# The last layer's weight conversion begins at step 9 of the experts instead of step 0

## The chip, the cores and the metric

One core of a Trainium2 chip runs the whole program. The metric is device time in microseconds (us), as the median of the runs that a table below gives. One further execution was recorded by the hardware profiler; all rows below are from it.

## The reference

Three stages follow one another. Sparse attention (4 batches, 8 heads, 576 rows, 64 columns) gives 2304 tokens of 512 numbers. A mixture of 8 experts sends each token to one expert (argmax of a gate) and applies two layers with a relu between, 512 to 1024 to 512. A last layer of two matrices, 512 to 2048 to 512, is shared by all tokens:

```python
def _moe2_ref(x, w_in, w_out) -> np.ndarray:
    h = x @ w_in
    g = h - np.tanh(h)
    return (g @ w_out).astype(np.float32)
```

`w_in` and `w_out` are float64. The kernel gets them as pairs of 32-bit words and makes float32 numbers of them on the chip. That making is the conversion which the change moves.

## The kernel before

The change touches the stage of the experts. It runs in steps, g = 0 to 71: nine passes of eight steps, one pass per expert and two for the second largest group (steps 8 to 23). A pass handles N = 256, 256, 288, 416, 384, 336, 320, 288 and 272 tokens in turn, and a step one eighth of the hidden width. The last layer's 96 steps follow (`GE` is 72, so its numbers are counted from there).

In a step the loop of `run` issues, in this order: the first-layer product of step g on TensorE (`h_exp`, L982, twelve matmuls, since each factor is split in a high and a low part); the relu, on ScalarE (L1017) and VectorE (L1018, the low part); whatever the table of `plan` holds for this step; then the second-layer product of step g-2 (`y_exp`, L1037). Each engine works through what it was given in the order of issue. Nothing overtakes.

The table holds:

- `gather_exp` (L999): rows of tokens by an indirect transfer that GpSimd issues, ten steps ahead of a pass.
- `trans` and `evac` (L959, L969, L973): the gathered rows are transposed by TensorE into PSUM and taken out by ScalarE (L969) and VectorE (L973), seven steps ahead, so at steps 1, 2 and 3 of the pass before. There is one PSUM bank "t" for it: a second transpose waits until L973 has read the first.
- `wload` and `wsplit` (L944 or L933, L950, L952): 512 KB of weights are loaded by the SP queue, cast by ScalarE and split, first-layer weights by VectorE on even steps, second-layer weights by GpSimd on odd ones. "raw" has four buffers.
- the tables of positions and gates (`route_late`, L523 and others), every second step from 8 to 30.
- `conv`, 32 times: half a block of the float64 words. Four jobs at steps g, g+3, g+4, g+5: load (SP, L1078), `bits` (VectorE: L1088, L1090, L1092), `sign` (ScalarE L1096, VectorE L1097, GpSimd L1099), store to `wscr` (SP, L1102). "cv" has three buffers. `conv` comes last in the table of a step.
- `"last"`: when the converted blocks are read back and split.

At the end of a pass `y_exp` copies its four results out (L1040), two by ScalarE and two by VectorE ("yo"). These copies are issued in the second step of the next pass, behind all that the table held for that step, and the pass after needs the banks one step later. "h" has two banks in PSUM: the first-layer product of step g+2 waits for L1018 of step g.

Of the kernel before, what the change touches and what calls it, by code (L numbers as in the profile page):

```python
# [863 lines left out]
class Mlp(Moe):  # L864
# [315 lines left out]
    def early(self):  # L1180
# [3 lines left out]


    TB = {"wl": (4, 5), "ws": (2, 3), "ga": 10, "tr": 7, "ev": 7,
          "last": ((-3, -2), (-1, 1), (-2, 0), (0, 2), (-1, 2), (0, 3), (1, 2), (4, 6), (-60, -55), (-53, -50), (-7,
                  -1), (-6, -4), (5, 10), (9, 11), (11, 12), (12, 14)), "x0": (12, 9, 7), "x": (14, 13, 8),
          "conv": (0, 1, 3, 5, 7, 10, 11, 13, 15, 16, 18, 20, 21, 23, 25, 28, 29, 32, 33, 35, 37, 38, 40, 42, 44, 46,
                  47, 51, 52, 54, 57, 57), "cv": (0, 3, 4, 5), "eng": "DPDPDPDPDPPDDDPP"}  # L1190

    def plan(self, K):
        at = self.at
# [82 lines left out]
```

## Times and profile before

| what | value |
|---|---|
| median of 3 runs | 1124.69 us (1124.59 to 1127.33) |
| profiled execution: its own time | 1123.74 us |
| profiled execution: span | 1122.0 us |
| TensorE matmul busy | 989.8 us, 88% |
| TensorE weight load busy | 916.7 us, 82% |
| VectorE busy | 901.3 us, 80% |
| ScalarE busy | 643.5 us, 57% |
| GpSimd busy | 716.9 us, 64% |

The span runs from the first to the last instruction; the execution's own time is 1.74 us more. Shares are means over the attention (to about 380 us), the experts (about 402 to 695 us) and the last layer. Shares say which engine has room; which wait ends last in a stretch is read from the timeline.

### The profile page before, as it was taken

To read this page: it belongs to the slowest core of one execution; us is meant where nothing else is said; L and a number is where in the kernel's file an instruction comes from. 1 tells how busy PE (TensorE), PEld (TensorE's weight loads), DVE (VectorE), ACT (ScalarE), POOL (GpSimd) and SP (SyncE) were. 2 spreads that over 40 slices of the span, in tenths; PEclk is the share of its full clock that TensorE was granted. 3 is DMA by queue.
4 is the path that set the end of the run, shared out by engine and by line. 5 is a ranking of instruction groups with operands and counts; after the bars stand their busy time and mean duration, and the time that the engine had idled before them with its cause. 6 is when DMAs were issued, how large, how long until landed. Compare 5 with 4: busy or idle time off the path is not lost.

```text
span 1122.0 us, 23396 instructions
## 1 busy us (share of the span) xinstructions
PE 989.8 (88%) x8729; PEld 916.7 (82%) x8729; DVE 901.3 (80%) x1600; ACT 643.5 (57%) x1207; POOL 716.9 (64%) x538
## 2 busy tenths in 40 slices
PE   4769698788887677999999998989999999999997
PEld 3669688777787567989999998877999999999986
DVE  4969687877679359885979876988988989898894
ACT  5768677667676044433445546665566666566662
POOL 3958667757766046555555657776776767677673
PEclk9789889989899679999999999999999999999999
DMA  7999999999999576686778875320010101000000
GB/s 176 172 190 201 218 198 204 214 176 192 201 171 177 130 244 208 236 281 216 250 248 278 283 254 192 112 85 8 36 29 20 46 10 36 19 29 1 13 17 29
DMA packets 249778, 162.68 MB, mean 145 GB/s; under 512 B 180122, under 2 KB 222508, under 8 KB 249661
## 3 DMA queue, kind: packets, MB, share of 16 engines
q1 hardware_dynamic: 245901, 150.36, 56.4%
q0 software_dynamic: 3312, 10.49, 2.7%
q8 instruction: 70, 1.15, 0.4%
q14 instruction: 47, 0.39, 0.1%
q10 hardware_dynamic: 448, 0.30, 0.1%
HBM read 85.08 MB, written 23.60 MB: 97 GB/s over the span
## 4 chain that ended last, share of the span: by engine, by line
PE 45%; DVE 13%; issue 3%; ACT 2%; DMA 1%; POOL 0%; DVEq 0%; POOLq 0%; SPq 0%; ACTq 0%
PE h L982 22%; PE y L1056 14%; PE y L1037 8%; DVE w L1162 2%; DVE w L1163 2%; DVE cv L1090 2%; DVE cm L1088 1%; DVE w L1164 1%; DVE w L1160 1%; DMA xr<-rows,idx 1%; DVE w L952 1%; DVE cm L1092 1%; PE t L959 1%; ACT w L950 1%; DVE hbuf L1018 0%
## 5 line engine op out<-in xcount | busy, mean ns | idle before, releaser
L233 POOL TENSOR_TENSOR e<-em,e 128x1536 f16<-128x1536 f32 (+1 forms) x53 | 155.6, 2936 | 89.1 <-ACT e L229 61.6
L263 PE MATMUL ops<-vv,et 128*128 128x64 bf16 (+1 forms) x1440 | 143.6, 202 | 9.7 <-DVE x L269 5.4
L263 PEld LDWEIGHTS <-et 128*128 128x128 f16 (+1 forms) x3680 | 134.9, 107 | 19.7 <-issue 8.4
L221 DVE SCALAR_TENSOR_TENSOR em<-sps,n,e 128x576 f32<-128x576 f32 x144 | 116.6, 810 | 40.6 <-ACT e L208 39.5
L1159 POOL TENSOR_SCALAR tm<-u 128x384 uint8<-128x384 f32 x80 | 117.3, 1466 | 49.9 <-ACT u L1155 49.3
L982 PE MATMUL h<-xa,w 128*128 128x256 f32 (+6 forms) x864 | 142.2, 315 | 7.0 <-DVE hbuf L1018 5.0
L1037 PE MATMUL y<-hbuf,w 128*128 128x256 f32 (+6 forms) x864 | 141.0, 312 | 5.6 <-DVE yo L1040 5.6
L263 PE MATMUL ops<-vr,et 128*128 128x64 bf16 (+1 forms) x2240 | 142.0, 201 | 0.0
L982 PEld LDWEIGHTS h<-xa,w 128*128 128x128 f32 x864 | 132.5, 197 | 9.1 <-DVE hbuf L1018 5.9
L229 ACT CAST e<-em 128x576 f16<-128x576 f32 x144 | 97.1, 675 | 64.8 <-DMA et<-e 60.6
L1037 PEld LDWEIGHTS y<-hbuf,w 128*128 128x128 f32 x864 | 128.0, 191 | 7.0 <-DVE yo L1040 6.6
L202 DVE TENSOR_REDUCE n<-sps 128x1 f32<-128x576 f32 x144 | 107.5, 747 | 29.9 <-PE sps L194 28.7
L952 POOL TENSOR_TENSOR w<-raw,w 128x1024 fp32r<-128x1024 f32 x36 | 91.6, 2545 | 60.6 <-ACT w L950 32.2
L1162 DVE SCALAR_TENSOR_TENSOR w<-y,w 128x384 f32<-128x384 f32 x96 | 124.1, 1293 | 0.0
L1155 ACT ACTIVATE u<-h 128x384 f32<-128x384 f32 x96 | 47.1, 491 | 119.8 <-PE h L982 119.7
L208 ACT ACTIVATE e<-sps,n 128x576 f32<-128x576 f32 x144 | 107.9, 749 | 13.1 <-DVE n L202 11.9
L982 PE MATMUL h<-xk,w 128*128 128x384 f32 x576 | 109.8, 339 | 0.4 <-DVE tm L1161 0.2
L982 PEld LDWEIGHTS h<-xk,w 128*128 128x128 f32 x576 | 103.1, 189 | 5.0 <-DVE tm L1161 0.5
L1176 POOL TENSOR_TENSOR gl<-w,gh 128x384 fp32r<-128x384 f32 x83 | 85.5, 1031 | 30.4 <-ACT gh L1175 30.3
L1017 ACT ACTIVATE hbuf<-h 128x256 fp32r<-128x256 f32 (+6 forms) x72 | 31.1, 432 | 125.5 <-PE h L982 125.5
L194 PE MATMUL sps<-ka,qa 128*128 128x288 f32 x320 | 86.1, 362 | 8.6 <-DVE em L221 4.3
L1056 PE MATMUL y<-w,gh 128*128 128x512 f32 x258 | 82.3, 400 | 5.6 <-DVE yo L1040 4.1
(217 smaller groups left out, 2296.3 us busy)
## 6 DMA issues: line engine op xcount, KB each, us to landing
raw<-in_moe_w_dram SPq DMA_DIRECT2D x64, 512.0 KB, 5.1
qb<-qa SPq DMA_DIRECT2D x30, 304.0 KB, 4.3
cv<-in_moe_w_in_dram SPq DMA_DIRECT2D x16, 512.0 KB, 4.7
cv<-in_moe_w_out_dram SPq DMA_DIRECT2D x16, 512.0 KB, 4.5
wscr<-cm SPq DMA_DIRECT2D x32, 256.0 KB, 2.4
raw<-wscr SPq DMA_DIRECT2D x16, 512.0 KB, 4.1
xw<-yT SPq DMA_DIRECT2D x24, 192.0 KB, 2.3
vv<-in_v_dram SPq DMA_DIRECT2D x8, 512.0 KB, 5.2
```

What stands on the lines that cost most here:

```text
L202: nc.vector.tensor_reduce(out=n[:, 0:1], in_=ps[:, :, 0:288], axis=AX.XY, op=ALU.max, negate=True)
L208: nc.scalar.activation(out=e, in_=ps[:, :, 0:288], func=AF.Exp, bias=n[:, 0:1])
L221: nc.vector.scalar_tensor_tensor(out=self.em[u, g][:, i].rearrange("p (a b) -> p a b", a=2), in0=ps[:, :, 0:288], scalar=n[:, 1:2], in1=e, ...
L229: self.nc.scalar.copy(self.e16[u, g][:, i, 0:S], self.em[u, g][:, i])
L233: eng.tensor_tensor(out=e16[:, r, S + 64:], in0=em[:, r, 0:512], in1=e16[:, r, 0:512], op=ALU.subtract)
L263: nc.tensor.matmul(o[q], lhsT=et[:, base + c, q], rhs=vb[a][:, j, c if c < 5 else c - 5, :], start=(n == 0), stop=(n == len(terms) - 1))
L952: (self.nc.gpsimd if pool else self.nc.vector).tensor_tensor(out=l, in0=raw, in1=h.bitcast(F32), op=ALU.subtract)
L982: self.nc.tensor.matmul(out, lhsT=a, rhs=b, start=(i == 0), stop=(i == len(parts) - 1))
L1037: nc.tensor.matmul(self.ys[d], lhsT=a[:, f % 2, s], rhs=b, start=(f == 0 and i == 0), stop=(f == 7 and i == 2))
L1056: nc.tensor.matmul(self.ys[m], lhsT=a[:, s], rhs=b[:, f % 2], start=(f == 0 and i == 0), stop=(f == 15 and i == 2))
L1159: nc.gpsimd.tensor_scalar(out=mk, in0=u, scalar1=RCUT * RCUT, scalar2=None, op0=ALU.is_gt)
L1162: V.scalar_tensor_tensor(out=w, in0=y, scalar=b, in1=w, op0=ALU.add, op1=ALU.mult)
```

## The change

Only numbers in the table `TB` are changed: the steps of the 32 conversions, and the steps at which the first two converted blocks are read back and split.

```diff
-          "last": (..., (4, 6), (-60, -55), (-53, -50), (-7,
+          "last": (..., (4, 6), (-51, -47), (-46, -43), (-7,
...
-          "conv": (0, 1, 3, 5, 7, 10, 11, 13, 15, 16, 18, 20, 21, 23, 25, 28, 29, 32, 33, 35, 37, 38, 40, 42, 44, 46,
-                  47, 51, 52, 54, 57, 57), "cv": (0, 3, 4, 5), "eng": "DPDPDPDPDPPDDDPP"}
+          "conv": (9, 10, 12, 13, 15, 16, 18, 19, 21, 23, 24, 26, 27, 29, 30, 32, 33, 35, 37, 38, 40, 41, 43, 44,
+                   46, 48, 49, 51, 52, 54, 55, 57), "cv": (0, 3, 4, 5), "eng": "DPDPDPDPDPPDDDPP"}
```

The two pairs of "last" are the load and the split of block 4 of `w_in` (before: steps 12 and 17, after: 21 and 25) and of block 4 of `w_out` (before: 19 and 22, after: 26 and 29). The first is split by VectorE, the second by GpSimd.

## Rows read from the trace of the kernel before

**Rows 1.** The page: the chain that ended last, by engine.
```profile
PE 45%; DVE 13%; issue 3%; ACT 2%; DMA 1%; POOL 0%; DVEq 0%; POOLq 0%; SPq 0%; ACTq 0%
```
**Rows 2.** Busy us by stretch (instructions in brackets), then granted clock and DMA.
```profile
core 0: us, PE busy (x) PEld busy (x) DVE busy (x) ACT busy (x) POOL busy (x), PEclk, DMA share, GB/s
421.13:449.50 28.37, 21.01 (x159) 20.15 (x158) 27.70 (x39) 12.37 (x26) 17.23 (x11) 0.94 0.64 211
...
461.01:490.26 29.25, 27.75 (x211) 26.91 (x209) 26.23 (x45) 12.78 (x27) 13.72 (x10) 1.00 0.80 263
...
503.34:567.03 63.69, 63.69 (x378) 62.91 (x376) 47.96 (x72) 28.83 (x51) 34.17 (x20) 1.00 0.72 237
567.03:600.88 33.85, 31.84 (x206) 31.27 (x206) 26.42 (x38) 15.95 (x29) 18.73 (x12) 1.00 0.82 279
```
**Rows 3.** Timeline of PE, steps 6 to 13: start, duration, idle before in brackets.
```profile
421.13 1.60 PE L982 MATMUL h<-xa,w 128*128 128x256 f32 x12
...
425.63 1.70 PE L982 MATMUL h<-xa,w 128*128 128x256 f32 x12 [1.47 <-DVE hbuf L1018]
...
434.37 0.63 PE L959 MATMUL t<-ident,xr 128*128 128x128 f32 x4 [1.28 <-DMA xr<-rows,idx]
...
442.67 0.79 PE L959 MATMUL t<-ident,xr 128*128 128x128 f32 x4 [4.61 <-issue]
443.11 2.91 PE L1037 MATMUL y<-hbuf,w 128*128 128x256 f32 x12
...
449.50 1.60 PE L982 MATMUL h<-xa,w 128*128 128x256 f32 x12
...
452.38 1.60 PE L982 MATMUL h<-xa,w 128*128 128x256 f32 x12
```
**Rows 4.** Timeline of DVE and POOL in the same stretch.
```profile
422.12 2.83 POOL L952 TENSOR_TENSOR w<-raw,w 128x1024 fp32r<-128x1024 f32 x1
...
422.75 2.50 DVE L1092 TENSOR_SCALAR cm<-cv 128x512 f32<-128x512 f32 x1
...
441.82 0.74 DVE L973 TENSOR_TENSOR xa<-t,xa 128x384 fp32r<-128x384 f32 x2
```
**Rows 5.** Tile cm: VectorE's four operations (min/median/max ns); last, its busy us, 408.87 to 663.45.
```profile
L1088 DVE TENSOR_SCALAR cm<-cv x32: 409/420/2648, 414.9 to 656.0; 128x512 uint32<-128x512 uint32 x32
L1090 DVE SCALAR_TENSOR_TENSOR cv<-cv,cm x32: 692/694/2879, 415.3 to 656.5; 128x512 uint32<-128x512 uint32 x32
L1092 DVE TENSOR_SCALAR cm<-cv x32: 426/428/2812, 416.1 to 657.2; 128x512 f32<-128x512 f32 x32
...
L1097 DVE SCALAR_TENSOR_TENSOR cm<-cv,cm x32: 673/682/3553, 420.0 to 660.6; 128x512 f32<-128x512 f32 x32
...
sum 254.58, PE 0.00 PEld 0.00 DVE 118.46 POOL 42.84; mean PE 0.00 PEld 0.00 DVE 14.81 POOL 5.36
```
**Rows 6.** Timeline of steps 22 to 26.
```profile
488.10 2.49 POOL L952 TENSOR_TENSOR we<-raw,we 128x1024 fp32r<-128x1024 f32 x1 [3.62 <-ACT we L950]
488.25 2.70 DVE L523 TENSOR_TENSOR keep<-keep,tok 128x324 f16<-128x324 f32 x1
...
494.04 2.76 DVE L1092 TENSOR_SCALAR cm<-cv 128x512 f32<-128x512 f32 x1
...
497.36 4.09 PE L982 MATMUL h<-xa,w 128*128 128x416 f32 x12 [2.49 <-DVE hbuf L1018]
...
503.34 2.44 PE L982 MATMUL h<-xa,w 128*128 128x416 f32 x12
```
**Rows 7.** Waits of PE from 403 to 690 us: total, times, longest.
```profile
PE y L1037 <- DVE yo L1040: 5.6, 4, 2.2
PE h L982 <- DVE hbuf L1018: 5.0, 4, 2.5
```
**Rows 8.** Timeline of PE and DVE at step 34.
```profile
543.71 2.35 PE L1037 MATMUL y<-hbuf,w 128*128 128x384 f32 x12
...
543.80 1.07 DVE L1040 COPY yo<-y 128x416 f32<-128x416 f32 x2
```

More of the change, by code (lines that the diff above doesn't have):

```diff
@@ L1186 @@
     TB = {"wl": (4, 5), "ws": (2, 3), "ga": 10, "tr": 7, "ev": 7,
-          "last": ((-3, -2), (-1, 1), (-2, 0), (0, 2), (-1, 2), (0, 3), (1, 2), (4, 6), (-60, -55), (-53, -50), (-7,
+          "last": ((-3, -2), (-1, 1), (-2, 0), (0, 2), (-1, 2), (0, 3), (1, 2), (4, 6), (-51, -47), (-46, -43), (-7,
                   -1), (-6, -4), (5, 10), (9, 11), (11, 12), (12, 14)), "x0": (12, 9, 7), "x": (14, 13, 8),
-          "conv": (0, 1, 3, 5, 7, 10, 11, 13, 15, 16, 18, 20, 21, 23, 25, 28, 29, 32, 33, 35, 37, 38, 40, 42, 44, 46,
-                  47, 51, 52, 54, 57, 57), "cv": (0, 3, 4, 5), "eng": "DPDPDPDPDPPDDDPP"}
+          "conv": (9, 10, 12, 13, 15, 16, 18, 19, 21, 23, 24, 26, 27, 29, 30, 32, 33, 35, 37, 38, 40, 41, 43, 44,
+                   46, 48, 49, 51, 52, 54, 55, 57), "cv": (0, 3, 4, 5), "eng": "DPDPDPDPDPPDDDPP"}
     def plan(self, K):
```

## The prediction

> **What bounds the kernel now.** I read the chain of waits first. TensorE has 45% of the chain and VectorE 13%, far ahead of ScalarE and DMA [rows 1]: the kernel goes at TensorE's pace, broken by places where TensorE waits for VectorE. Then the stretches of the expert stage, the only stage in which conversions run [rows 2]. From 503.34 to 567.03 us TensorE is busy for all of the 63.69 us, and VectorE's 47.96 us of work cost nothing. From 421.13 to 449.50 us, steps 6 to 11, it is the other way round: VectorE is busy for 27.70 of 28.37 us and TensorE for 21.01. So the question is which waits fall in such stretches, and whether the conversion is in front of them.
>
> The timeline of TensorE in that stretch shows three waits [rows 3]: 1.47 us before step 7 (for L1018), 1.28 us before the first transposes (for gathered rows), 4.61 us before the second ones. After the last, y of step 8 takes 2.91 us, where a product of this width takes 1.60: the granted clock of the stretch is 0.94 [rows 2]. VectorE's and GpSimd's rows name the cause [rows 4]. The wait of 1.47 ends after L1092, a conversion's operation, which took 2.50 us beside GpSimd's split of 2.83 us. The wait of 4.61 us is put down to "issue", but it ends at 442.67 us, just as L973 ends (441.82 + 0.74 = 442.56): the single bank "t" was not read yet, since L973 stood in VectorE's queue behind conversions and the table of positions. The gather that TensorE waited 1.28 us for is issued by GpSimd, whose queue had conversion multiplies in front of it.
>
> **The change part by part.** Price of a conversion first. Its four VectorE operations have medians of 0.420, 0.694, 0.428 and 0.682 us, 2.22 together; their real total is 118.46 us for 32 conversions, 3.70 each [rows 5]. The 1.48 us between is time in which they stood blocked beside GpSimd.
>
> Counting `bits` per pass, before: 3, 4, 5, 4, 4, 5, 4, 3, 0; after: 0, 3, 5, 5, 5, 6, 5, 3, 0. Most of the conversions stay within a step or two of their place. In effect five leave steps 3 to 10 and come in at steps 12 to 15, 29, 33, 44 to 46 and 52.
>
> *Steps 6 to 11, removed.* The five that leave take 5 x 3.70 = 18.5 us of VectorE out of steps 3 to 11. What TensorE needs for steps 6 to 11: a step takes 452.38 - 449.50 = 2.88 us [rows 3], six make 17.28; three groups of transposes at 443.11 - 442.67 = 0.44 make 1.32; together 18.6. They took 28.37. So up to 9.8 us go. What is late next: the table of positions still stands at step 8, ahead of L973, and one blocked operation costs 2.5 us [rows 4]; with two of them left the gain would be 4.8. I take 9.5, near the upper end, because VectorE's 27.70 us shrink by well over a third and no other engine is near full (GpSimd 17.23) [rows 2].
>
> *Step 25.* TensorE waits 2.49 us for L1018 and then runs its next product at 4.09 us instead of 2.44, together 4.1 us [rows 6]. In front of L1018 of step 24 stood the `bits` of step 23, whose L1092 took 2.76 us, and before that L523, which took 2.70 us beside a GpSimd split of a "we" block. Both move: that split goes to step 29, and these `bits` to step 22. Then L523 should cost about 0.7 (the longest unblocked one of rows 5), so VectorE gains 2.0 and pays 1.54 for `bits` earlier; the L1018 of step 23 comes no later, and nothing long is left before that of step 24. Bounds: nothing gained, or 4.1. I take 4.1, since both blockers are named and gone. The other block's split, 1.2 us of VectorE unblocked, comes into step 25 instead of 17, in a pass where a product takes 2.44 us and not 1.60; taken as hidden.
>
> The Trainium skill ("SBUF — State Buffer", section "SBUF: two separate sides") says that VectorE and GpSimd share a port pair as an exclusive lock: the first to start holds it for its whole instruction and the other fully blocks. The trace agrees: L523 started 0.15 us after the split and ended 0.36 us after it [rows 6]. By that rule each moved conversion may pay a whole split more, 5 x 2.49 = 12 us of VectorE, if its new place is beside one; were all of it on the path, the sum below would come to about +1.5. That speaks against the change, and the third rival prices the same thing from rows.
>
> *Steps 12 to 17.* Three `bits` (13, 14, 16) become four (12, 13, 15, 16), with the gate's table at step 12 and the one-hot tables at 14 and 16. Besides the two waits counted above, TensorE waits 1.0 us for L1018 in the stage, in two places [rows 7]. Bounds: -1.0 (they vanish) to +3.7 (a whole conversion on the path). I take +1.0, since from 461.01 to 490.26 VectorE is 90% busy and TensorE still lost only 29.25 - 27.75 = 1.5 us [rows 2]: h's two banks absorb about a step.
>
> *Step 33.* A new `bits` stands just ahead of the "yo" copies. Before, these ended at 544.9 us; y of the next pass began at 543.71 and wants the freed bank half way through its 2.35 us, at 544.9, by when the first of the two copies had 0.5 us in hand [rows 8]. The new `bits` cost 1.54 unblocked, 3.0 blocked, so +1.0 to +2.5. I take +1.2, since the `sign` of an earlier conversion (0.68) leaves step 32 in return.
>
> *Steps 43 to 49.* One more conversion: VectorE goes from 26.42 to 30.1 of 33.85 us, 78 to 89% [rows 2]. The copies at step 49 may come later: 0 to the longest of the four waits for "yo", 2.2 us [rows 7]. I take +0.7.
>
> *Steps 29, 52, 60.* Covered by TensorE at 29 (503 to 567 us, above); at 60 two conversions in one step become one each at 58 and 60: -0.2.
>
> *The queues.* 32 loads and 32 stores stay. The SP queue loses five of each in steps 0 to 15. Later, load n+3 comes only four steps after load n ten times (never before), so it waits in SP for GpSimd's multiply of that same step, and weight loads queue behind it; the block of step 21 also holds one of four "raw" buffers up to step 25. Neither wait is in the trace. Bounds: 0 to one wait of 2.5 us with its slow restart, as at step 25 [rows 6]; I take 0, because weights are loaded two steps or more before they are split.
>
> Sum: -9.5 - 4.1 + 1.0 + 1.2 + 0.7 - 0.2 = -10.9. The profiled execution took 1123.74 us (span 1122.0 plus 1.74), so 1112.8; the median of the runs is 0.95 us above the profiled one, so 1113.8. The last layer only shifts, as its order is unchanged.
>
> **The rivals.**
>
> 1. *The wait comes back in steps 12 to 17.* The gate's table, a split and the first two `bits` fall together there, and L973 of step 17 is late as that of step 9 was: +3.7 for the conversion and 1.6 for a slow restart (4.09 - 2.44, rows 6), instead of +1.0. Then 1113.8 + 4.3 = 1118.1. For: four in five steps. Against: no expert weights are split in steps 14 to 21.
> 2. *Step 25 stays.* `bits` at 22 only push L1018 of step 23, and the product for the tables takes an h bank as well. No 4.1: 1117.9. Against: L523 is free there.
> 3. *Blocked conversions ahead of the copies; slower.* With 89% in VectorE, `bits` at steps 33, 41, 49 and 57 each begin beside a GpSimd split, and TensorE waits 2.5 us and restarts slowly, 1.65 more, at each of the four: 16.6, against 5.6 now for four such waits [rows 7], so +11.0 in place of my +1.9. With 25 still there and 12 to 17 at its upper end: -9.5 + 3.7 + 11.0 = +5.2, that is 1129.9. It decides from three slow restarts on. For: three of the four have `bits` in that place already and wait. Against: only one of the four is new.
> 4. *The change does not free steps 6 to 11.* The 4.61 us are not VectorE's queue but the gather or weights, so only the 1.47 go: -1.5 - 4.1 + 2.7 = -2.9, that is 1121.8. For: "issue" as the named cause. Against: L973 ends 0.1 us before.
>
> **How the numbers follow.** Forecast 0.55 (its own range 1110 to 1117), rivals in order 0.15, 0.14, 0.07, 0.09. A measurement here can tell about 0.3%, 3.4 us, from no change. Faster, below 1121.3: 0.55 + 0.14 + 0.11 of the first rival = 0.80; slower 0.07; the same 0.13. Low end: 9.8 + 4.1 + 1.0 + 0.2 gained and nothing lost, 1109.6. High end: rival 4's time, 1122, which leaves out the third.
>
> **What would show it.** Right: h of step 12 some 18.6 us after h of step 6; no wait of 4.61 us before a transpose; the product of step 25 at 2.44 us; VectorE well under full in steps 6 to 11; a "yo" wait near step 34. Wrong: a TensorE wait over 2 us with a slow restart in steps 12 to 17 or at 33, 41, 49 or 57, or SP standing at a conversion load while ScalarE waits for weights.

## The result, and the profile after

The changed kernel is slower: a median of 1134.67 us (1133.09 to 1136.46, 4 runs) beside 1124.64 us (1124.08 to 1127.33) for the kernel before in the same session, a ratio of 1.009 with a 95% interval from 1.0066 to 1.0115. Forecast were 1113.8 us and "faster", with a range of 1110 to 1117; the change goes the other way. The profiled execution took 1133.09 us with a span of 1131.4, so it shows 9.4 us of the 10.0.

The chain that ended last, by engine, from the page; [rows 1] had 45% for TensorE, 13% for VectorE and 1% for DMA:

```profile
PE 37%; DVE 16%; DMA 4%; issue 3%; ACT 2%; POOL 1%; SPq 0%; DVEq 0%; POOLq 0%; ACTq 0%
```

The page's list by line says what the 4% are: `DMA wscr<-cm`, the store of a converted half block. It is not among the lines that the page lists for the kernel before's chain.

Busy us by stretch, columns as in [rows 2]; the stretches are steps 6 to 11, then 32 to 39, 40 to 47, 48 to 55 and 56 to 63:

```profile
core 0: us, PE busy (x) PEld busy (x) DVE busy (x) ACT busy (x) POOL busy (x), PEclk, DMA share, GB/s
423.82:442.50 18.68, 18.68 (x158) 18.51 (x157) 9.77 (x23) 10.08 (x22) 10.12 (x6) 1.00 0.74 246
527.89:565.23 37.34, 35.18 (x205) 34.71 (x205) 32.63 (x44) 17.42 (x30) 23.43 (x15) 1.00 0.84 274
565.23:600.35 35.12, 32.08 (x205) 31.23 (x205) 26.89 (x37) 16.15 (x29) 19.26 (x11) 1.00 0.78 257
600.35:635.65 35.30, 31.93 (x206) 30.76 (x205) 32.25 (x39) 15.84 (x29) 20.87 (x13) 0.95 0.79 259
635.65:671.26 35.61, 30.76 (x206) 29.51 (x205) 27.08 (x42) 16.58 (x30) 18.94 (x12) 0.90 0.80 272
```

Steps 6 to 11 take 18.68 us, all of it TensorE's; before they took 28.37 [rows 2]. In the four passes below TensorE stands 2 to 5 us each.

A sum of the parts is had from the start of h (L982) in the first step of a pass, counted from h of step 0, less the same in the kernel before. This table stands for all kernels below; minus is earlier. Each row is one execution, while the ratios further down are medians of several; where the two differ, the text says so. The last two columns are the end of the span counted in the same way, and the time in the trace at which step 0 itself begins (402.06 in the kernel before).

| kernel | step 16 | 32 | 40 | 48 | 56 | 64 | 72 | end | step 0 at |
|---|---|---|---|---|---|---|---|---|---|
| after | -7.5 | -7.0 | -4.6 | -3.3 | +1.2 | +5.0 | +5.0 | +6.6 | 404.86 |
| e1, after again | -7.5 | -6.9 | -4.6 | -2.5 | +2.1 | +5.3 | +5.2 | +6.7 | 407.17 |
| e2, splits only | -0.5 | -4.2 | -4.2 | -4.2 | -4.2 | -4.3 | -4.3 | -3.9 | 402.01 |
| e3, five without work | -9.9 | -10.4 | -10.4 | -10.4 | -10.4 | -10.6 | -10.5 | -10.2 | 402.67 |
| e6, third half of cm | -8.2 | -9.9 | -7.8 | -6.4 | -2.5 | -0.9 | -1.0 | -2.3 | 404.95 |
| e4, bits behind copies | -8.2 | -4.2 | -2.7 | +1.2 | +1.8 | +3.0 | +2.9 | +4.0 | 405.34 |
| e5, before, bits behind | +0.4 | -0.4 | -0.4 | -2.7 | -3.3 | -2.3 | -2.4 | -0.6 | 403.79 |
| e8, both | -8.2 | -10.0 | -10.0 | -9.7 | -7.2 | -6.0 | -6.0 | -5.7 | 402.65 |
| e7, conversions only | -8.2 | -5.3 | -1.6 | 0.0 | +5.3 | +7.6 | +7.6 | +8.0 | 405.38 |
| e9, every second step | -8.5 | -13.5 | -13.5 | -15.8 | -16.8 | -20.5 | -9.4 | -4.1 | 409.05 |
| e14, the same, odd | -8.8 | -12.4 | -12.2 | -13.8 | -13.8 | -17.1 | -7.0 | -1.4 | 404.39 |
| e10, even to 66 | -8.0 | -11.6 | -11.6 | -11.6 | -11.5 | -10.8 | +0.2 | +2.6 | 409.48 |
| e11, dense in 24 to 39 | -8.3 | -12.6 | -8.2 | -3.9 | -4.8 | -8.5 | -0.5 | -1.3 | 406.28 |
| e12, dense, to 59 | -8.7 | -12.9 | -8.7 | -5.4 | -0.6 | -1.8 | +1.8 | +0.3 | 406.88 |
| e13, from step 1 | -0.6 | -5.1 | -5.1 | -7.4 | -8.4 | -12.0 | -5.0 | -2.9 | 406.58 |
| e15, five before step 4 | +5.3 | +0.4 | +0.4 | -1.9 | -2.9 | -6.6 | +0.9 | -0.7 | 405.81 |
| e16, cadence from 25 | +0.5 | -3.6 | -3.6 | -5.9 | -6.9 | -2.3 | -2.3 | -0.7 | 407.01 |

At step 12 the changed kernel is 9.8 us early. From there to step 64 it loses 14.8 us, the last layer 1.6 more, and the experts begin 2.8 us later: -9.8 + 14.8 + 1.6 + 2.8 = +9.4.

**The early gain.** Timeline of TensorE, steps 6 to 12 (the view ends inside the last product); it answers to [rows 3]:

```profile
423.82 1.60 PE L982 MATMUL h<-xa,w 128*128 128x256 f32 x12
...
433.90 0.60 PE L959 MATMUL t<-ident,xr 128*128 128x128 f32 x4
...
437.21 0.60 PE L959 MATMUL t<-ident,xr 128*128 128x128 f32 x4
...
442.50 0.76 PE L982 MATMUL h<-xa,w 128*128 128x256 f32 x5
```

No row of that stretch has an idle time before it: the waits of 1.47, 1.28 and 4.61 us are gone.

**The waits that came.** Waits of TensorE, then of VectorE, 405 to 695 us (total, times, longest); the first view answers to [rows 7]:

```profile
PE y L1037 <- DVE yo L1040: 11.0, 5, 3.2
PE h L982 <- DVE hbuf L1018: 5.8, 6, 1.5
```

```profile
DVE cm L1088 <- DMA wscr<-cm: 17.6, 8, 4.2
```

In the kernel before the last wait occurs once, for 0.4 us. VectorE now stands 17.6 us in front of the first operation of `bits` until an earlier store has landed, and TensorE's waits for the copies of y double from 5.6 to 11.0 us. One place shows how the two hang together. Timeline of all engines, steps 56 to 58:

```profile
641.15 1.38 POOL L1099 TENSOR_TENSOR cm<-cv,cm 128x512 f32<-128x512 f32 x1 [1.43 <-issue]
...
642.55 0.35 SPq L1078 DMA_DIRECT2D cv<-in_moe_w_out_dram  x1
643.10 0.38 SPq L944 DMA_DIRECT2D raw<-in_moe_w_dram  x1
643.53 0.49 SPq L1102 DMA_DIRECT2D wscr<-cm  x1
...
648.79 0.90 DVE L1088 TENSOR_SCALAR cm<-cv 128x512 uint32<-128x512 uint32 x1 [2.12 <-DMA wscr<-cm]
...
650.80 0.88 DVE L1040 COPY yo<-y 128x320 f32<-128x320 f32 x2
...
651.34 1.81 PE L1037 MATMUL y<-hbuf,w 128*128 128x288 f32 x6 [3.15 <-DVE yo L1040]
...
652.95 3.08 PE L982 MATMUL h<-xa,w 128*128 128x288 f32 x12
```

Read from the top: GpSimd finishes a multiply at 642.53. At once SP issues a conversion's load, which had waited for that cv buffer, then a load of weights that was queued behind it, and only then the store of the half that has just been made. The store lands 5.1 us later, at 648.67 by the chain of waits. `cm` has two halves, one for each half of a block, so the next conversion but one writes the same half: its L1088 stood at the head of VectorE's queue until the store had landed. Behind it stand the rest of `bits` and the two copies of y of a pass that has ended. TensorE waits 3.15 us for these, and its next product takes 3.08 us, where one of this width takes 1.75 at full clock.

Where a half is used again three steps later, its `bits` stand one step behind the store. By the two lists that is so for 12 of 30 conversions before and for 27 of 30 after. The stores whose landing the trace tells (19 of 32 before, 8 of 32 after) land later too. DMA issues, with size and the median us from issue to landing of these, first of the kernel before, then after:

```profile
wscr<-cm SPq DMA_DIRECT2D x32, 256.0 KB, 2.4
```

```profile
wscr<-cm SPq DMA_DIRECT2D x32, 256.0 KB, 5.3
```

What stands right ahead of a store goes with it: nine of these 27 have a load of 512 KB issued at most 1.5 us ahead and landed after 4.2 to 7.4 us; seventeen have no transfer there and landed after 2.0 to 4.2 us, but for one of 5.3.

**Step 25.** Timeline of steps 21 to 25, to set beside [rows 6]:

```profile
482.27 0.43 DVE L1088 TENSOR_SCALAR cm<-cv 128x512 uint32<-128x512 uint32 x1 [3.30 <-DMA wscr<-cm]
...
485.31 0.49 DVE L523 TENSOR_TENSOR keep<-keep,tok 128x324 f16<-128x324 f32 x1
...
489.20 3.09 DVE L1097 SCALAR_TENSOR_TENSOR cm<-cv,cm 128x512 f32<-128x512 f32 x1
...
492.85 2.54 PE L982 MATMUL h<-xa,w 128*128 128x416 f32 x12 [1.19 <-DVE hbuf L1018]
```

L523 is free, at 0.49 instead of 2.70 us, and the product after it runs at nearly full pace (2.54 us for 2.44), but 1.19 us of the wait are left, and TensorE waits 1.12 us just before for the product of the tables. Two things stand in VectorE's queue ahead of these: L1088 of step 21 has waited 3.30 us for a store, and L1097 in step 23 took 3.09 us beside a split of GpSimd's.

### The profile page after: what moved, and what is told of

Its sections match the earlier page's. It is cut to its first block, busy times and chain, and to the rows that moved or that the text cites. A ratio compares the mean times of both kernels' runs of the same rounds, so it can differ in the third digit from the quotient of the medians.

```text
span 1131.4 us, 23377 instructions
## 1 busy us (share of the span) xinstructions
PE 991.8 (88%) x8729; PEld 915.8 (81%) x8729; DVE 896.9 (79%) x1600; ACT 644.1 (57%) x1207; POOL 714.8 (63%) x538
## 3 DMA queue, kind: packets, MB, share of 16 engines
q8 instruction: 70, 1.15, 0.4%
## 4 chain that ended last, share of the span: by engine, by line
PE 37%; DVE 16%; DMA 4%; issue 3%; ACT 2%; POOL 1%; SPq 0%; DVEq 0%; POOLq 0%; ACTq 0%
PE h L982 18%; PE y L1056 14%; PE y L1037 5%; DMA wscr<-cm 4%; DVE w L1162 3%; DVE cv L1090 2%; DVE w L1163 2%; DVE w L1164 1%; DVE w L1160 1%; DVE cm L1097 1%; DVE cm L1088 1%; DVE w L952 1%; DVE cm L1092 1%; POOL cm L1099 1%; ACT t L1157 1%
## 5 line engine op out<-in xcount | busy, mean ns | idle before, releaser
L982 PE MATMUL h<-xa,w 128*128 128x256 f32 (+6 forms) x864 | 142.2, 315 | 8.2 <-DVE hbuf L1018 5.8
L982 PEld LDWEIGHTS h<-xa,w 128*128 128x128 f32 x864 | 131.8, 196 | 10.9 <-DVE hbuf L1018 7.3
L1037 PEld LDWEIGHTS y<-hbuf,w 128*128 128x128 f32 x864 | 127.2, 190 | 12.9 <-DVE yo L1040 12.4
L208 ACT ACTIVATE e<-sps,n 128x576 f32<-128x576 f32 x144 | 107.8, 748 | 13.2 <-DVE n L202 12.2
L982 PE MATMUL h<-xk,w 128*128 128x384 f32 x576 | 110.6, 340 | 0.4 <-DVE tm L1161 0.2
L982 PEld LDWEIGHTS h<-xk,w 128*128 128x128 f32 x576 | 103.9, 191 | 5.0 <-DVE tm L1161 0.5
L1099 POOL TENSOR_TENSOR cm<-cv,cm 128x512 f32<-128x512 f32 x32 | 42.9, 1341 | 73.5 <-issue 30.0
```

Source lines behind the costliest of these rows:

```text
L208: nc.scalar.activation(out=e, in_=ps[:, :, 0:288], func=AF.Exp, bias=n[:, 0:1])
L982: self.nc.tensor.matmul(out, lhsT=a, rhs=b, start=(i == 0), stop=(i == len(parts) - 1))
L1037: nc.tensor.matmul(self.ys[d], lhsT=a[:, f % 2, s], rhs=b, start=(f == 0 and i == 0), stop=(f == 7 and i == 2))
```

## The experiments

Ratios are to the kernel before on the same chip, with 95% intervals. Times are medians.

**e1: the changed kernel again.**

> The changed kernel once more, unchanged, to see what repeats from execution to execution. Both theories: 1133 to 1136 us. If the 2.8 us by which the experts began later in the first profile of the changed kernel (404.86 against 402.06 us) is chance, the start moves by some us again, and the steps from 12 on lose the same amounts: VectorE's waits of L1088 for the store out of cm at 15 to 20 us.

1134.98 us, ratio 1.0073 (1.0048 to 1.0097). The same waits are there: 18.5 us in seven for the store, 11.2 us in five for the copies. They belong to the schedule, not to one execution.

**e2: the splits alone.**

```diff
 # kernel before
-          (-60, -55), (-53, -50)
+          (-51, -47), (-46, -43)
```

> The kernel before with only the two read-backs of block 4 moved (steps 21/25 and 26/29); all conversions at their old steps. Theory W (the conversions stand closer, so L1088 waits for the store of the conversion that used the same half of cm, and what is queued behind it is late): the splits don't matter, 1121 to 1126 us, L1088 waiting under 2 us. Theory D (too much VectorE work in the later steps): 1.2 us of work moved from step 17 to 25, 1123 to 1127. Theory P (the moved splits do the harm): 1130 or more.

1122.5 us, ratio 0.9957 (0.9941 to 0.9973), faster than both kernels. Timeline:

```profile
486.58 0.49 DVE L523 TENSOR_TENSOR keep<-keep,tok 128x324 f16<-128x324 f32 x1
...
493.52 2.54 PE L982 MATMUL h<-xa,w 128*128 128x416 f32 x12 [0.32 <-DVE hbuf L1018]
```

The wait of 2.49 us [rows 6] falls to 0.32 and the slow product of 4.09 us to 2.54: 2.17 + 1.55 = 3.7 us at that place. The table has the same 3.7 from step 16 to 32, and it stays to the end (the 0.5 before that is there at step 8, ahead of anything that was moved). The splits do this alone; no `bits` had to move for it, and Theory P is out.

**e3: the first five conversions do no work.** Their five half blocks are not converted; zeros are stored in their place, all loads and stores stay.

```diff
 # kernel before
+                self.conv(*CORD[n], work=n > 4)   # bits and sign return at once for n < 5
```

> The kernel before with its schedule, but the first five conversions do no arithmetic: their words are loaded, and zeros stored in their place, so these five half blocks of the last layer's weights are not converted. The gain of steps 6 to 11 alone, with no work added later. All theories: steps 6 to 12 in about 18.6 us and not 28.4, and 9 to 11 us less than before, 1114 to 1116, if what is won at step 12 is kept to the end. If the later waits come from the steps running earlier against DMA rather than from added conversions, less is kept: 1118 to 1124.

1115.91 us, ratio 0.9912 (0.9888 to 0.9936). All 10 us come up to step 16 and nothing of it goes again. So what the changed kernel loses later is the price of where its conversions now stand, not an early start that collides with something. (ScalarE's and GpSimd's part of the five is left out here too, so this run does not say whose queue it was.)

**e6: a third half for cm; e4: bits behind the copies; e8: both; e5: the second alone on the kernel before.**

```diff
 # e6, e8: changed kernel
-            st["m"] = self.cm.bitcast(F32)[:, 512 * h:512 * h + 512]
+            st["m"] = self.cm[self.nm % 3]     # the two halves and one further tile, in turn
 # e4, e8: changed kernel; e5: kernel before
-                at(g + o, fn)
+                at(g + o + (0.5 if o == 3 else 0), fn)   # bits after the y product and its copies
```

> The changed kernel with a third half block for the result of a conversion, so a half is used again by the third conversion after and not by the second. Theory W: L1088's waits for stores fall from 17.6 us in eight to under 3 us, and most of what the later steps lost comes back: 1120 to 1128 us. Theory D: VectorE's queue is as long as before and the waits for yo stay (11 us in five): 1131 to 1136.

> The changed kernel with one thing different: the three VectorE operations called bits are issued at the end of their step, behind the product y and the copies out of it, and not before them. Theory O (what the later steps lose is that conversions stand in VectorE's queue ahead of the yo copies at the turn of a pass): the waits for yo fall from 11 us in five to under 4, without a slow restart, and the time to 1122 to 1128 us, although L1088 still waits for stores. Theory D (too much VectorE work, wherever it stands): the waits move to L1018, 1131 to 1136. Theory W (the waits for stores): 1130 to 1135.

> The kernel before with the same edit: bits at the end of their step, behind the copies. Theory O: its waits for yo (5.6 us in four, and one slow restart of 1.6) fall under 2 us, the waits of steps 6 to 11 stay: 1118 to 1122 us. Theory D: within 2 us of the kernel before, the waits for yo replaced by waits for L1018.

> The changed kernel with both: a third half block for the results and bits behind the copies. Theories W and O together: what is won by step 12 (10 us) is kept but for 2 to 4 us in steps 12 to 16, and the 4 us of the splits come on top: 1112 to 1119 us. Theory D: VectorE's queue is as long as before, and waits for L1018 take the place of those for yo: 1125 to 1131.

| | cm with two halves | with three |
|---|---|---|
| bits as in the changed kernel | 1.009 and 1.0073 | 1.0035 (1.0011 to 1.0059) |
| bits behind the copies | 1.0033 (1.0007 to 1.0058) | 0.9986 (0.9964 to 1.0008) |

From a mean of 1.0082, each edit brings 0.0047 to 0.0049, some 5.4 us, and both together 0.0096, 10.8 us. An estimate from the intervals gives each of these some 3 us either way. Counted from step 0 to the end, the traces say 8.9 us for the first, 2.6 for the second and 12.3 for both. So both edits bring something and together some 11 to 12 us; how that is to be shared out is not settled. On the kernel before, the second edit brings nothing (0.9992, 0.9969 to 1.0015): its waits for the copies fall from 5.6 to 0.6 us, but those for L1018 grow from 5.0 to 6.7. With the third half no wait of L1088 for a store is left; with the bits behind the copies it stays, and its longest gets longer. VectorE's waits in e4:

```profile
DVE cm L1088 <- DMA wscr<-cm: 18.5, 7, 5.9
```

TensorE's in e8, with both:

```profile
PE h L982 <- DVE hbuf L1018: 6.3, 7, 1.5
...
PE y L1037 <- DVE yo L1040: 0.8, 1, 0.8
```

The copies are no longer waited for, and L1018 a little more. But the median of e8 is no faster than the kernel before: of the 10 us that its trace is ahead at step 40, it loses 4 up to step 64, and of the 5.7 us that are left at the end the median shows 1.6 (see "Open").

**e7: the changed conversions, block 4 split near its old steps (20 and 22).**

```diff
 # changed kernel
-          (-51, -47), (-46, -43)
+          (-55, -52), (-53, -50)
```

> The changed kernel with the read-backs of block 4 put back near their old place (loads at steps 17 and 19, splits at 20 and 22), so that only the conversions are moved. The splits alone were worth 4.2 us from step 26 on. If the two parts add up: the wait at steps 24 and 25 of about 4 us is back, and the time is 2 to 5 us above the changed kernel, 1135 to 1139 us. If the harm came from the splits beside the dense conversions: 1126 to 1131.

1133.79 us, ratio 1.0074 (1.0048 to 1.01): the medians show no difference from the changed kernel, and the 2 to 5 us of the expectation did not come. In the trace the moved splits are worth 2.4 us from step 16 to 32, and 1.4 at the end, instead of e2's 3.7.

**e9: one conversion at every second step, 9 to 71; e14: the same one step earlier, 8 to 70; e10: spread evenly from 9 to 66.** All three are the changed kernel with another list.

```diff
-          "conv": (9, 10, 12, 13, 15, 16, ...)
+          "conv": (9, 11, 13, ..., 71)             # e9
+          "conv": (8, 10, 12, ..., 70)             # e14
+          "conv": (9, 11, 13, 15, 16, 18, ..., 66) # e10
```

> The changed kernel with its 32 conversions spread further: one begins at every second step, 9, 11, 13 and so on to 71, so a half of cm is reused after four steps each time, and no bits stand at the second step of a pass, ahead of the yo copies. The start, the early gain and the two splits of block 4 are the changed kernel's. Theory (the loss after step 12 lies in three places: cm reused too early, bits ahead of the copies, and too many conversions per pass): no wait of L1088 for a store, no yo wait over 1 us, step 12 some 9.8 us early, step 26 some 11.8, and 10 or more still there at the end of the experts: 1113 to 1117 us, a ratio of 0.989 to 0.993. Rival (the five conversions cost TensorE's stretches the same wherever they stand): no better than the third half with the copies in front, 1120 to 1126, a ratio of 0.995 to 1.0. Second rival (the late conversions hold up the last layer, whose own loads and splits begin at step 69): the gain is whole at step 64 and falls by 3 us or more between step 64 and the first steps of the last layer.

> The every-second-step kernel shifted by one step, 8, 10, 12 to 70: the same number per pass and the same reuse of cm, but all bits at odd steps, beside GpSimd's splits, and four in a pass of which one stands at its second step, ahead of the yo copies. Theory (place): 1.3 us more of VectorE for each conversion and waits for yo of 1 to 2 us at the turn of most passes, 8 to 14 us behind the every-second-step kernel at step 64; a ratio of 1.005 to 1.013. Rival (number per pass): within 3 us of the every-second-step kernel at each step, a ratio of 0.998 to 1.003.

> The same, spread evenly from step 9 to step 66: mostly every second step, but bits stand at the second step of a pass four times (25, 41, 49, 65), and a half of cm is reused after three steps seven times. Theory of the three places: the waits come back in part, some 1 us at each of those four pass turns and at a few stores; 3 to 5 us behind the every-second-step kernel, 1117 to 1121 us, a ratio of 0.992 to 0.996. Rival (only the number of conversions per pass counts, 4 to 5 here as before): the same as the every-second-step kernel to within its interval. Second rival (the pass turns and stores are nothing, and the spreading gains nothing): 1120 to 1126.

e9: 1125.33 us, 0.9999 (0.9981 to 1.0017). e14: 1125.74, 0.9998 (0.9982 to 1.0015). e10: 1130.42, 1.0046 (1.0023 to 1.0068). Stretches from step 32 to 63 and 64 to 71, e9 and then e14:

```profile
525.64:649.95 124.31, 123.72 (x818) 122.61 (x817) 85.05 (x142) 60.91 (x111) 73.16 (x42) 1.00 0.85 283
649.95:685.40 35.45, 28.38 (x194) 27.49 (x193) 32.24 (x38) 17.70 (x29) 22.65 (x12) 0.90 0.78 268
```

```profile
522.09:648.70 126.61, 124.40 (x817) 122.56 (x817) 112.88 (x143) 61.92 (x112) 70.62 (x42) 1.00 0.82 281
648.70:683.13 34.43, 27.59 (x195) 26.95 (x193) 31.82 (x34) 15.61 (x26) 21.48 (x12) 0.90 0.76 258
```

With four conversions per pass TensorE is busy for 123.72 of 124.31 us, and the kernel is 20.5 us ahead at step 64: the term for the density is real, and larger than I thought. Between steps 32 and 64 it gains 7.0 us on the kernel before, of which 6.1 are that kernel's own waits for the copies (2.01, 0.74 and 2.23 us, and 1.15 in a slow product). But the 20.5 are in part work put off: six of the 32 `bits` come at step 64 or later. Then steps 64 to 71 take 35.45 us instead of 24.3: the last conversions meet the last layer's scaling and splitting of x, and VectorE is 91% busy. The second rival in e9's expectation came true, with 11.1 us ("3 or more"). The theory's "10 or more at the end of the experts" are 9.4 at step 72; 5.3 of these go in the last layer, where TensorE waits 10.3 us between 690 and 735 us, 7.4 of them for ScalarE (in the kernel before 6.5), and the median shows nothing of the 4.1 that are left.

e14 was to tell the place from the number. VectorE's busy time in the four operations of all 32 conversions (first figure after the length of the window), e9 and then e14:

```profile
405.00:735.00 330.00, 93.95 (x128) 0.95 0.71 235
```

```profile
405.00:735.00 330.00, 140.19 (x128) 0.97 0.69 233
```

That is 2.9 us for a conversion whose `bits` stand at an even step, and 4.4 at an odd one, beside GpSimd's split. VectorE has 27.8 us more to do between steps 32 and 64 in e14, and yet TensorE loses only 2.3 us by it. My theory (the place decides, 8 to 14 us) is wrong and its rival nearly right (3.4 us apart at step 64, where it said 3): the price of a conversion counted little here, with VectorE 89% busy. `bits` stand ahead of the copies at every turn of a pass in e14, and the copies cost TensorE 4.0 us in four waits up to step 63, no more than in the kernel before. e10 ends 5.1 us behind e9, near the 3 to 5 expected, but above all three forecast times. It reuses a half of `cm` after three steps ten times, not seven, has half its `bits` at odd steps and five in some passes, and loses 0.8 us from step 32 to 63 where e9 gains 7.0. Which of these does it was not tried one by one.

**e11 and e12: dense where a step is longest.** With the third half of cm: every second step from 9 to 23, then 12 conversions in steps 24 to 39, then every second step from 41 to 63 (e11), or 12 in steps 41 to 59 and none later (e12).

```diff
+          "conv": (9, 11, ..., 23, 24, 25, 27, 28, 29, 31, 32, 33, 35, 36, 37, 39, 41, 43, ..., 63)
```

> Every second step from 9 to 23 (8 conversions), 12 in steps 24 to 39, where a step of TensorE is longest (416 and 384 tokens), then every second step from 41 to 63; no bits at the second step of a pass, ahead of the yo copies; and the third half for cm, so that it is reused after four steps or more. Theory (places decide, and the every-second-step kernel lost its gain of 20.5 us only to the conversions that began in steps 61 to 71, beside the last layer's own preparation): nearly as far ahead at step 64, 16 us or more, of which at most 4 go up to step 72; 1110 to 1114 us, a ratio of 0.986 to 0.991. Rival (an expert stage with 32 conversions after step 9 loses about 10 us wherever they stand): ahead by 10 or less at step 64 and 4 to 6 at the end, as the third half with the copies in front: 1119 to 1124.

> As the one before, but 12 instead of 8 conversions in steps 41 to 59 and none later: every second step again save three pairs of neighbours in steps 43 to 49. Theory: no loss from step 64 to 72 (under 1 us), but 3 to 6 us less ahead at step 64 than the kernel that goes to 63, from waits before L1018 and the copies in steps 43 to 50; 1110 to 1115 us, a ratio of 0.987 to 0.991, so about the same in sum. Rival (the end at 63 was harmless and the three pairs are too): the same at every step.

1125.96 us, 1.0005 (0.9988 to 1.0022), and 1129.95, 1.0048 (1.0026 to 1.0069). Both theories failed. e11 loses 4.4 us in steps 32 to 39, with six `bits` in the pass, and 4.3 in the next, which has four. VectorE had been busy for only 47.96 of 63.69 us in steps 26 to 39 [rows 2], which I took for room; a conversion costs 3 to 4 us of it, and at 37.20 of 39.31 us TensorE waits again for the transposes, 2.67 us in that pass and 3.90 in the next. e12 waits 12.2 us for them in four passes and is 1.8 us ahead at step 64, where e11 is 8.5.

**e13: every second step from 1 to 63; e15: five before step 4, then 9 to 61; e16: the first 14 as before the change, then every second step from 25, the last two together at 57.**

```diff
+          "conv": (1, 3, 5, ..., 63)                                      # e13
+          "conv": (-5, -3, -1, 1, 3, 9, 11, ..., 61)                      # e15
+          "conv": (0, 1, 3, 5, 7, 10, ..., 23, 25, 27, 29, ..., 57, 57)   # e16
```

> One conversion at every second step from 1 to 63, so all bits stand at even steps, beside no split of GpSimd; the splits of block 4 as in the changed kernel. Theory (the place beside a split sets the price: bits 3.6 us at odd steps, 2.2 at even ones, as the traces so far show): steps 3 to 11 hold four conversions as cheap as 3.0 us instead of five at 3.7, so 3 to 6 us early at step 12, some 14 or more at step 64, of which 3 to 8 go up to step 72: 1113 to 1119 us, a ratio of 0.990 to 0.995. Rival (only the number per pass counts): four in the first steps instead of five bring 2 us, and the splits 4.2: about as the kernel with the splits only, 1119 to 1123.

> Five conversions begin at steps -5, -3, -1, 1 and 3, beside the gather and the first transposes, where VectorE waits 4.6 us for ScalarE, and the others at every second step from 9 to 61; bits all at even steps. Theory (the price is low at even steps, steps 6 to 11 are free, and the end at 61 meets little of the last layer's preparation): 6 to 9 us early at step 12, 14 to 18 at step 64, under 5 lost up to step 72: 1109 to 1115 us, a ratio of 0.986 to 0.991. Rival (conversions ahead of step 0 wait for their loads and hold VectorE's queue up): the first product of the experts 2 to 5 us later, and the whole no better than 1118.

> The first 14 conversions at the steps of the kernel before (0 to 23), the other 18 at every second step from 25 to 57, the last two together at 57 as there; the splits of block 4 as in the changed kernel. Theory (four conversions per pass, all bits at even steps and none at the turn of a pass, cost TensorE nothing; only conversions that begin after 57 gave it back): as the splits alone up to step 32 (4.2 us early), 10 to 12 at step 64 and the same at step 72 and the end: 1112 to 1116 us, a ratio of 0.989 to 0.992. Rival (the gain of the cadence between 32 and 64 was work put off, and comes back wherever the last conversions stand): 4 us at step 72, as the splits alone, 1119 to 1122.

1125.76 us, 0.9998 (0.9979 to 1.0018); 1127.26, 1.0012 (0.9985 to 1.0038); 1125.68, 0.9985 (0.9957 to 1.0012). All three theories missed. In e13 four cheap conversions in steps 3 to 11 cost nearly as much as the five before: step 12 is 2.7 us early and not 9.8, and TensorE waits 4.5 us for the same transposes again. In e15 the gain at step 12 doesn't come, and step 16 is 5.3 us late. TensorE's waits there, 396 to 455 us:

```profile
PE t L959 <- DVE xa L973: 3.1, 1, 3.1
PE t L959 <- issue: 2.6, 1, 2.6
```

e16 holds 6.9 us at step 56 and gives 4.6 back at once, where the last two conversions stand together in step 60. Timeline:

```profile
658.23 0.43 DVE L1088 TENSOR_SCALAR cm<-cv 128x512 uint32<-128x512 uint32 x1 [1.83 <-DMA wscr<-cm]
...
660.27 3.25 PE L982 MATMUL h<-xa,w 128*128 128x288 f32 x12 [4.26 <-DVE hbuf L1018]
```

The same wait for a store stands ahead of the L1018 that TensorE needs: by this list the last conversion uses its half again two steps after the one that filled it, so its `bits` fall in the very step of the store. So e16 does not settle whether the gain of the cadence would last. Of all that was run with the whole computation, the splits alone (e2) are the only one whose interval lies below the kernel before.

## Why the prediction was wrong

**Right.** Steps 6 to 11: 18.68 us, forecast 18.6, and 9.8 us at step 12 against 9.5. Without the five conversions' work it is the same 10 us (e3). That four cheaper ones bring the wait of 4.5 us back (e13) says that their place in the queue counts, and not only the sum of 18.5 us. The mechanism of step 25 was right also: 4.1 forecast, 3.7 measured in e2, though the splits did it all: of the two blockers named, L523 counted and the `bits` of step 23 did not. In the changed kernel the gain is eaten (7.5 us early at step 16, 7.0 at step 32).

**The step that failed first: "The queues ... I take 0, because weights are loaded two steps or more before they are split."** I had seen that a load waits in SP for GpSimd's multiply, and asked only who else is late for weights. The store that SP issues behind that load was not followed any further, and neither was the buffer it empties: `cm` has two halves, conversion n+2 needs the half of n, and its L1088 stands in VectorE's queue ahead of all that TensorE needs. I counted the buffers of "cv" and "raw" and never those of `cm`, though the one half per h stands in `load`. It costs 17.6 us of VectorE in eight waits, one of them the 3.30 us ahead of step 25, and taking it away brings some 5.4 us of the time (e6). The Trainium skill ("DMA: Bandwidth & Descriptors", section "Queues, rings and completion order") says that transfers issued by one engine are taken up in order on each DMA engine, and that the signal of a finished one comes only after all earlier writes of that DMA engine. The trace is in line with it: the store issued behind two loads landed after 5.1 us, where the median before was 2.4. My upper bound, one wait of 2.5 us and its slow restart (4.1 us), was too small as well.

**The terms for the later steps: +1.0, +1.2, +0.7 and -0.2, together +2.7.** Measured, without the step-25 gain: +2.3 in steps 12 to 15, +2.4 in 32 to 39, +9.6 in 40 to 63; and in steps 16 to 31, where e2 gains 3.7, the changed kernel loses 0.5. Two causes are shown. One is the store, above. The other is `bits` ahead of the copies at the turn of a pass, some 5.4 us (e4), at the place that the third rival named: the waits for "yo" went from 5.6 to 11.0 us, and those of 2.77 and 3.15 us were followed by products of 3.22 and 3.08 us, a sign of being wrong that the prediction had named for steps 49 and 57. Its excess over my terms was 9.1 us, so its size was about half, with two slow restarts (one of them there before) and not three; and where it had the blocking beside GpSimd, the longest wait has a store in front. I gave it 0.07, and of all rivals its 1129.9 came nearest. That the place alone is not enough is seen in e14. The rest is argued: e8, with both other causes gone, still loses 3.9 us from step 32 to 63, in which e9 gains 7.0. The two differ in the number of conversions per pass (five and six for four) and in how evenly they are spaced, and no run parts these.

**What I took for cover was none.** "Covered by TensorE at 29 (503 to 567 us)" rested on TensorE being busy throughout. A stretch in which TensorE never waits says that VectorE is in time as things stand, not that it has room: e11 put work there and lost 4.4 us in one pass.

**The price of a conversion.** The 3.70 us of [rows 5] are roughly a mean over two prices, 2.9 and 4.4 (e9 and e14). Here are the same operations after; in sum the four take 112.29 us instead of 118.46:

```profile
L1088 DVE TENSOR_SCALAR cm<-cv x32: 407/419/2619, 450.8 to 662.9; 128x512 uint32<-128x512 uint32 x32
L1090 DVE SCALAR_TENSOR_TENSOR cv<-cv,cm x32: 692/1184/2782, 451.3 to 663.3; 128x512 uint32<-128x512 uint32 x32
L1092 DVE TENSOR_SCALAR cm<-cv x32: 426/427/2781, 452.0 to 664.0; 128x512 f32<-128x512 f32 x32
L1097 DVE SCALAR_TENSOR_TENSOR cm<-cv,cm x32: 669/683/3477, 452.7 to 664.8; 128x512 f32<-128x512 f32 x32
```

So the blocking beside GpSimd did not grow, and the loss is not there. The Trainium skill ("SBUF — State Buffer", section "SBUF: two separate sides") says that the engine which starts first holds the shared pair of ports for its whole instruction (on VectorE's side for the kinds of operation that it lists). The trace agrees in the two prices. The 12 us of VectorE that I derived from that rule as a threat did not come, and the 27.8 us by which e14 exceeds e9 were worth 2.3 us of TensorE.

**The other rivals.** The first (a wait in steps 12 to 17) named a real place: TensorE waits 1.52 us for L1018 in step 15, and 1.50 us before a transpose at 466.75 us. But no slow restart follows, and the loss was +2.3, nearer my +1.0 than its +5.3. The second (step 25 stays) was wrong in e2, but near the truth for the changed kernel: the product for the tables and step 25 both wait there, though for a store and a blocked L1097 and not for `bits` at 22 alone. The fourth (no relief of steps 6 to 11) was wrong.

**Open.** "The last layer only shifts" left out that the experts begin later. Up to step 0 all kernels but e15 issue the same instructions in the same order, and yet h of step 0 began at 402.0 to 403.8 us in the four profiles with the old list of conversions and at 402.7 to 409.5, on average 406.2, in the thirteen others. The difference grows little by little through the attention. One profile of each can't tell chance from cause, and none of the runs was made for it. For chance: e16 and e2 have the same schedule up to step 26, and h of step 0 began 5.0 us apart. Against it: the medians. Compared with the kernel before, the times of e2, e3 and e5, by their ratios, are within 1 us of what their traces show from step 0 on; those of the thirteen others are on average 2.5 us worse than that (1.0 better to 6.2 worse). So some 2 us of the loss, and of what e6, e8 and e9 fail to show in their medians, may lie ahead of the experts, where no explanation was found.

## What to carry to other kernels

When work is moved in a schedule written out by hand, follow each buffer that it writes to the instruction that uses it next, in steps: a store that is issued one step before its buffer is needed is late as soon as the queue in front of it is. Before a stretch is called free, add the moved work to the engine that is to take it and see what then stands in front of the bottleneck's next need. How many pieces fall in a pass, and how they are spaced, counted here for more than what each costs (e9 and e14). And where one edit holds two moves, the small one alone may be the gain: e2 alone beat the kernel before, by 0.4%.

## What the runs showed of the hardware

- A store of 256 KB landed 2.0 to 4.2 us after its issue where SP had issued nothing in the 1.5 us ahead (16 of 17 landings), and 4.2 to 7.4 us after it with a load of 512 KB there (nine landings).
- Not each wait of TensorE is followed by slow products: after 2.02 us (in the pass from step 40 of the changed kernel) the next product took 2.01 us, as at full clock; after 2.77 and 3.15 us the next ones took 3.22 and 3.08, where they take 1.92 and 1.75 at full clock. The granted clock of the two passes with these was 0.95 and 0.90. In the kernel before 2.23 us (step 58) were enough: the next product took 2.90 for 1.75.
- VectorE's 27.8 us of added busy time in steps 32 to 63 (e14 against e9, the blocking beside GpSimd) cost TensorE 2.3 us, a twelfth of that.
